# Batch 1's start in a spectral filter with a GELU layer: the filters' return, the weight sums and the tables at other places

## The chip, the cores and the metric

The kernel runs on one core of a Trainium2 chip. The metric is the device time of one execution in microseconds (us); lower is better. Before the change the median of three runs is 760.87 us (760.04 to 762.06).

## The reference

```python
X = np.fft.rfft(x, axis=1)                    # x: (8, 3008, 256)
Y = X * (filt_r + 1j * filt_i)[None, :, :]    # filters: (1505, 256)
y = np.fft.irfft(Y, n=3008, axis=1).astype(np.float32)
h = y.reshape(8 * 3008, 256) @ w_in           # w_in: (256, 2048)
g = 0.5 * h * (1.0 + erf(h / sqrt(2)))
out = g @ w_out                               # w_out: (2048, 256)
```

Each of eight batches is filtered along its 3008 positions in the frequency domain; the result then passes a layer of 2048 GELU units.

## The kernel before

**Two halves that run together.** The GELU layer works on 47 row tiles of 512 rows. Each tile has 16 slots; slot `s` belongs to tile `s // 16`. In every slot the loop at lines 865 to 872 first calls what the dictionary `at` holds for it, then one sixteenth of the previous tile's second product (`mm2` for the first and last tile, `mm2_seven` otherwise), then one sixteenth of this tile's first product (`mm1`, two matmuls of 512 columns and a GELU on ScalarE, ACT in the profile). Within each engine instructions run in the order in which the program issues them; no planner reorders them. So `put(slot, f, ...)` at lines 820 to 857 is the order of the work.

Batch 0 is filtered ahead of slot 0, by routines of its own. Batches 1 to 7 are filtered by calls that `put` has spread over the slots, one batch while the tiles of the one before go through the layer. Batch 1 must be ready at slot 80.

**The transform.** 3008 = 47 x 64, done in two stages each way:

- `s1` (four chunks of a batch): matmuls with table `T1s`; four evacuations into `a_sb` (three buffers); four DMA writes to the DRAM tile `R1` (R in the profile).
- `r1` (four chunks): reads `R1` back, transposed, into `b_sb` (three buffers), once all writes of `s1` have landed.
- `s2` (12 units `p`): two matmuls with `T2p`, then a product with the filter tile `F` on VectorE (DVE), 1024 elements wide. Unit p reads k = 2p and 2p + 1 of `F`. Below this product is called p(0) to p(11).
- `s3` and `s3_out` (three groups): inverse stage with table `U`, evacuated to `v_sb`, written to `R2`.
- `r2`, `s4`: read back as `d_sb`, last stage with table `T4a`, written to the ring `y_sb` that `mm1` reads.

**Filters.** Batch 0 needs `F` in one arrangement, the later batches in another. `save_filters` wrote `F` to the DRAM tile `Fd`; `load_filters_again` brings it back in the new arrangement, k = 0 to 7 as eight transfers of 128 KB (F1 below) and k = 8 to 23 as eight of 256 KB (F2). Each goes to 16 partitions. Units 0 to 3 read F1, units 4 to 11 F2.

**Queues.** All these transfers are issued by SyncE (SP) in program order. GpSimd (POOL) issues the loads of `x`, which `load_next` places at slot 25 for batch 2, and of `w_out`. It also computes tables: `table_2_parities` (`T2p`), `table_u_pick`, `table_4_rows`, `weights_4`, then the 24 products of `table_4_all` (`T4a`), which follow `table_4_factors` (three small matmuls and three evacuations on ACT).

**Seven products.** `mm2_seven` takes seven products of quarters in place of eight. For that it needs sums of quarters of `w_out` (`weight_sums`, into `w_sums`; once, before slot 36) and, per tile, sums of quarters of `g` (`sums_1`, `sums_2`, `sums_3` at lines 627, 633 and 640, on VectorE). The two PSUM banks `ps_o` are used in turn, and lines 670 to 680 read them on VectorE. Product m covers n = 16 m to 16 m + 15; slot s of a tile covers n = 7 s to 7 s + 6. Product m = 2 reads the sum of line 633, second half from n = 36.

For batch 1 the slots come from line 829: chunk c of `s1` at 0, 4, 8, 12, `r1` at 15, unit p of `s2` at 25 + 12 (p // 4) + int(2.5 (p % 4)), `r2` at 62, `s4` from 70.

Of the kernel before, what the change touches and what calls it, by code (L numbers as in the profile page):

```python
# [30 lines left out]
class _Mix:  # L31
# [343 lines left out]
    def s1(self, b, c):  # L375

        nc = self.nc
        if c == 0:
            self.st[b, "R1"] = self.dram.tile([NB, 48, 256], BF16, tag="R1", name="R1")
        a = self.pa.tile([128, 2, 4, 256], BF16, tag="a", name="a_sb")  # L380
        x = self.st[b, "x"]
        ps = [[self.bank("ps_s1", "h" if i == h == 0 else "f") for h in range(2)] for i in range(2)]
        for i in range(2):
            for r in range(2):
                for h in range(2):
                    w = 8 * c + 4 * r + 2 * i
                    nc.tensor.matmul(ps[i][h][64 * r:64 * r + 64, :], lhsT=self.T1s[64 * h:64 * h + NA],  # L387
                                     rhs=x[64 * h:64 * h + NA, w:w + 2, :], start=True, stop=True)
        for i in range(2):
            for h in range(2):  # L390
                self._evac(a[:, h, 2 * i:2 * i + 2, :].rearrange("p a b -> p (a b)"), ps[i][h], "act" if h else False)
        o = self.st[b, "R1"].rearrange("n q c -> q n c")
        for r in range(2):
            for h in range(2):
                w = HB * h + 8 * c + 4 * r
                nc.sync.dma_start(out=o[:, w:w + 4, :], in_=a[64 * r:64 * r + 48, h])
# [209 lines left out]
    def weight_sums(self):  # L606

        w = self.w_out_sb.rearrange("p (i k) (n o) -> p k n i o", k=2, n=2)
        q, tt = self.w_sums, self.nc.gpsimd.tensor_tensor
        for o, a, b, op in ((q[:, 0], w[:, 0, 1], w[:, 0, 0], ALU.subtract), (q[:, 1], w[:, 1, 1], q[:, 0], ALU.add),  # L610
                            (q[:, 2], w[:, 1, 1], w[:, 0, 1], ALU.add), (q[:, 3], w[:, 1, 0], q[:, 1], ALU.subtract)):
            for i in range(0, 8, 2):
                tt(out=o[:, i:i + 2], in0=a[:, i:i + 2], in1=b[:, i:i + 2], op=op)

    def quarters(self, t):

# [77 lines left out]
def kernel(  # L694
# [9 lines left out]
    m = _Mix(ctx, tc, x, filt_r, filt_i, moe_w_in, moe_w_out, out)  # L704
# [4 lines left out]
    g = m.small  # L709
    wide = ctx.enter_context(ExitStack())  # L710
    m.psum(wide, w=(2, 1), m=(1, 1), n=(5, 1))
    act = "act"
# [107 lines left out]
    def put(slot, f, *a):  # L820
        at.setdefault(slot, []).append((f, a))

    def first(b):
        return (b * S // TCH) * 16

    for b in range(1, B):
        hi = first(b)
        if b == 1:
            s1, n1, r1, s2, n2, group, r2, s4, n4 = 0, 4, 15, 25, 2.5, 12, 62, 70, 0.62
        else:  # L830
            s1, n1, r1, s2, n2, group, r2, s4, n4 = hi - 94, 3.7, hi - 80, hi - 71, 3.4, 14, hi - 25, hi - 17, 1
        unit = lambda p: s2 + group * (p // 4) + int(n2 * (p % 4))
        for u in range(16):
            put(s4 + int(u * n4), m.s4, b, u // 2, u % 2)
        for c in range(4):
            put(s1 + int(c * n1), m.s1, b, c)
            put(r1 if c < 3 else unit(3) + 1, m.r1, b, c)
            put(r2 if c < 3 else s4 + int(4 * n4) + 1, m.r2, b, c)
        for p in range(12):
            put(unit(p), m.s2, b, p)  # L840
            if p % 4 == 3:
                put(unit(p) + 3, m.s3, b, p // 4)
                put(unit(p) + 4, m.s3_out, b, p // 4, 1)
        if b + 1 < B:
            for i in range(8):
                put(unit(i + 2) if b > 1 else 25, m.load_next, b, i + 2, i // 2, i % 2)

    put(0, m.table_2_parities)
    put(1, m.table_u_pick, g)
    put(1, m.table_4_rows, g)  # L850
    put(1, m.weights_4, g)
    put(10, m.load_filters_again, 0, 8)
    put(16, m.load_filters_again, 8, 16)
    put(4, m.weight_sums)
    put(12, m.table_4_factors, g)
    put(14, m.table_u)
    put(15, m.table_4_all, g)
    seven = range(1, NT - 1)
    for t in seven:
        for i, s in enumerate((12, 13, 15, 17)):  # L860
# [43 lines left out]
```

## Time and profile before

| | TensorE | VectorE | ACT | GpSimd |
|---|---|---|---|---|
| busy, us of 758.5 | 741.2 | 581.4 | 547.6 | 111.6 |
| instructions | 8388 | 1043 | 967 | 207 |

| stretch, us | TensorE busy | VectorE busy | ACT busy | GpSimd busy | DMA share | GB/s |
|---|---|---|---|---|---|---|
| 38 to 52 (slots 0 to 15) | 11.20 of 14 | 6.09 | 12.95 | 7.54 | 1.09 | 203 |
| 52 to 64 | 9.93 of 12 | 0.99 | 6.38 | 11.84 | 0.84 | 184 |
| 64 to 82 | 17.45 of 18 | 13.22 | 10.01 | 17.06 | 1.02 | 164 |
| 82 to 98 | 13.17 of 16 | 15.32 | 8.66 | 6.00 | 0.88 | 212 |
| 98 to 114 | 15.09 of 16 | 12.54 | 11.13 | 0 | 0.33 | 81 |
| 300 to 500 | 199.80 of 200 | 161.68 | 148.77 | 15.12 | 0.49 | 119 |

A stretch is a piece of time counted from the start of the profiled execution. DMA share is the mean busy share of the 16 DMA engines; it can pass 1 a little where packets overlap. A matmul's end is modelled in the profile, so a TensorE that is busy throughout is not necessarily at its peak, but a gap in it is a gap. The profile numbers lines as the kernel before has them.

### The profile page before, as it was taken

To read this page: it belongs to the slowest core of one execution; us is meant where nothing else is said; L and a number is where in the kernel's file an instruction comes from. 1 tells how busy PE (TensorE), PEld (TensorE's weight loads), DVE (VectorE), ACT (ScalarE), POOL (GpSimd) and SP (SyncE) were. 2 spreads that over 40 slices of the span, in tenths; PEclk is the share of its full clock that TensorE was granted. 3 is DMA by queue.
4 is the path that set the end of the run, shared out by engine and by line. 5 is a ranking of instruction groups with operands and counts; after the bars stand their busy time and mean duration, and the time that the engine had idled before them with its cause. 6 is when DMAs were issued, how large, how long until landed. Compare 5 with 4: busy or idle time off the path is not lost.

```text
span 758.5 us, 20181 instructions
## 1 busy us (share of the span) xinstructions
PE 741.2 (98%) x8388; PEld 519.3 (68%) x8388; DVE 581.4 (77%) x1043; ACT 547.6 (72%) x967; POOL 111.6 (15%) x207
## 2 busy tenths in 40 slices
PE   8988899999999999999999999999999999999998
PEld 4835567666777667666677666766677766777776
DVE  7935888799677986889777897779977799666562
ACT  7885567766787677867778667876678767777773
POOL 7969600021000210002000120001200000000000
PEclk9999999999999999999999999999999999999999
DMA  9999935555624745347525465254562432501011
GB/s 147 221 191 172 197 107 130 148 120 124 140 78 126 159 112 113 100 131 169 119 75 141 139 132 127 79 165 111 105 168 65 140 92 81 129 29 57 29 57 57
DMA packets 91500, 90.71 MB, mean 120 GB/s; under 512 B 7632, under 2 KB 78416, under 8 KB 91088
## 3 DMA queue, kind: packets, MB, share of 16 engines
q1 hardware_dynamic: 83024, 73.43, 36.2%
q0 software_dynamic: 8384, 16.00, 13.9%
q8 instruction: 65, 1.06, 0.6%
q14 instruction: 27, 0.22, 0.1%
HBM read 57.15 MB, written 48.23 MB: 139 GB/s over the span
## 4 chain that ended last, share of the span: by engine, by line
PE 85%; DVE 7%; DMA 4%; issue 1%; ACT 1%; POOL 0%; SPq 0%; DVEq 0%; ACTq 0%; POOLq 0%
PE ps_h L569 38%; PE ps_o L657 35%; PE ps_s L455 3%; PE ps_s L427 2%; DVE p L413 2%; DVE s_sb L627 2%; PE ps_s L410 2%; PE ps_s L387 2%; DMA b_sb<-R 2%; PE ps_o L596 1%; DMA R<-a_sb 1%; DMA x_sb<-in_x_dram 1%; PE ps_c L517 1%; ACT y_sb L295 1%; DVE ost L680 1%
## 5 line engine op out<-in xcount | busy, mean ns | idle before, releaser
L572 ACT ACTIVATE g_sb<-ps_h 128x512 f16<-128x512 f32 x752 | 448.2, 599 | 191.1 <-PE ps_h L569 188.7
L569 PE MATMUL ps_h<-y_sb,w_in_sb 128*128 128x512 bf16 (+3 forms) x1600 | 448.2, 368 | 1.3 <-ACT g_sb L572 0.8
L657 PEld LDWEIGHTS <-g_sb 128*128 128x128 f16 x2880 | 190.3, 98 | 81.7 <-issue 16.9
L657 PEld LDWEIGHTS <-s_sb 128*128 128x128 f16 x2160 | 147.3, 98 | 51.3 <-issue 3.3
L569 PEld LDWEIGHTS <-w_in_sb 128*128 128x128 bf16 x1600 | 125.2, 98 | 9.3 <-issue 3.6
L657 PE MATMUL ps_o<-w_sums,g_sb 128*128 128x128 f16 x1440 | 125.0, 219 | 2.2 <-DVE t_sb L673 1.5
L657 PE MATMUL ps_o<-w_sums,s_sb 128*128 128x128 f16 x1440 | 124.5, 219 | 0.0
L627 DVE TENSOR_TENSOR s_sb<-g_sb 128x1024 f16<-128x1024 f16 x180 | 121.4, 697 | 0.0
L413 DVE TENSOR_TENSOR p<-ps_s,F 128x1024 bf16<-128x1024 f32 x84 | 102.6, 1221 | 23.2 <-PE ps_s L410 15.8
L657 PE MATMUL ps_o<-w_out_sb,g_sb 128*128 128x128 f16 x1440 | 118.4, 219 | 0.4
L118 POOL COPY gate<-p 1x1 bf16<-1x1 bf16 x40 | 19.4, 484 | 415.3 <-DVE p L413 415.3
L633 DVE TENSOR_TENSOR g_sb<-s_sb,g_sb 128x1024 f16<-128x1024 f16 x90 | 62.3, 693 | 1.1
L657 PE MATMUL ps_o<-w_out_sb,s_sb 128*128 128x128 f16 x720 | 62.2, 219 | 0.0
L640 DVE TENSOR_TENSOR s_sb<-g_sb 128x1024 f16<-128x1024 f16 x90 | 61.5, 683 | 0.0
L299 DVE TENSOR_SCALAR y_sb<-ps_s 128x376 bf16<-128x376 f32 x56 | 30.6, 546 | 28.9 <-PE ps_s L455 28.9
L297 DVE CAST a_sb<-ps_s 128x512 bf16<-128x512 f32 x56 | 36.1, 686 | 18.6 <-PE ps_s L387 15.4
L455 PEld LDWEIGHTS <-d_sb 96*128 96x128 bf16 x448 | 31.2, 98 | 26.4 <-issue 1.9
L675 DVE TENSOR_TENSOR t_sb<-t_sb,ps_o 128x256 f32<-128x256 f32 x45 | 18.7, 416 | 38.5 <-PE ps_o L657 38.5
L672 DVE TENSOR_TENSOR ost<-t_sb,ps_o 128x256 f32<-128x256 f32 x45 | 18.9, 419 | 31.2 <-PE ps_o L657 31.2
L680 DVE TENSOR_TENSOR ost<-t_sb,ps_o 128x256 f32<-128x256 f32 x90 | 33.7, 416 | 6.8 <-PE ps_o L657 6.8
L455 PE MATMUL ps_s<-T4a,d_sb 96*128 96x94 bf16 x448 | 37.1, 206 | 1.0 <-DMA d_sb<-R 0.9
L410 PE MATMUL ps_s<-b_sb,T2p 128*128 128x256 bf16 x168 | 32.3, 274 | 2.1 <-DMA b_sb<-R 2.1
(149 smaller groups left out, 524.3 us busy)
## 6 DMA issues: line engine op xcount, KB each, us to landing
out_dram<-ost SPq DMA_DIRECT2D x93, 256.0 KB, 2.7
x_sb<-in_x_dram POOLq DMA_DIRECT2D x64, 188.0 KB, 3.6
R<-a_sb SPq DMA_DIRECT2D x112, 96.0 KB, 2.2
b_sb<-R SPq DMA_DIRECT2D x28, 384.0 KB, 4.4
R<-v_sb SPq DMA_DIRECT2D x84, 128.0 KB, 2.4
d_sb<-R SPq DMA_DIRECT2D x56, 192.0 KB, 3.9
F<-Fd SPq DMA_DIRECT2D x8, 256.0 KB, 12.1
Fd<-F SPq DMA_DIRECT2D x1, 1536.0 KB, 9.9
```

The source lines that it names most:

```text
L297: self.nc.vector.tensor_copy(out=out, in_=in_)
L299: self.nc.vector.tensor_scalar(out=out, in0=in_, scalar1=scale, scalar2=None, op0=ALU.mult)
L410: nc.tensor.matmul(ps[:, 256 * i:256 * i + 256], lhsT=self.T2p[:, k].rearrange("p a b c d -> p (a b c d)"), rhs=self.st[b, "b", k // 6][:, ...
L413: nc.vector.tensor_tensor(out=w, in0=ps.unsqueeze(1).to_broadcast([128, 2, 512]), in1=self.F[:, :, 2 * p:2 * p + 2, :].rearrange("p t a b ...
L455: nc.tensor.matmul(ps[:, 94 * i:94 * i + 94], lhsT=d[:, (grp % 2) * 4 + i, 128 * half:128 * half + 128], rhs=self.T4a[:, 4 * grp + i], sta ...
L569: nc.tensor.matmul(ps[:, o:o + n], lhsT=self.w_in_sb[:, dc, jc * 128:jc * 128 + 128], rhs=self.ring[:, dc, off:off + n], start=(dc == 0), ...
L572: nc.scalar.activation(out=self.st["g", t][:, jc, :], in_=ps, func=AF.Gelu)
L627: self.nc.vector.tensor_tensor(out=self.st["s", t][:, i:i + 2], in0=a, in1=b, op=ALU.subtract)
L633: self.nc.vector.tensor_tensor(out=a21[:, k], in0=self.st["s", t][:, k, 0], in1=a22[:, k], op=ALU.add)
L640: self.nc.vector.tensor_tensor(out=self.st["s4", t][:, k], in0=a12[:, k], in1=s2[:, k], op=ALU.subtract)
L657: nc.tensor.matmul(ps[:, (m + 1) % 2, sub, :], lhsT=a[:, i, 128 * sub:128 * sub + 128], rhs=b[:, i], start=i == 0, stop=i == 7)
L680: v(out=c(h, 1 - h), in0=tt, in1=p, op=ALU.add)
```

## The change

It moves work of batch 1's start. F1 goes from slot 10, between the writes of chunks 2 and 3 of `s1`, to slot 13, behind all sixteen writes; F2 goes one slot later. `weight_sums` goes from GpSimd (16 pieces) to VectorE (4 whole ones) and from slot 4 to 17. In `s1` of batch 1 a third evacuation of each chunk goes from ACT to VectorE. GpSimd's small tables that the factors need come ahead of `T2p`, the factors go from slot 12 to 7 and `table_u` and `table_4_all` to 11. Forward and inverse stage of batch 1 start three slots earlier: `s2` at 22, `r2` at 59, `s4` at 67, the last a little more widely spread (0.75 slots apart instead of 0.62). It is for bringing the writes and the forward stage forward and for taking load off GpSimd and ACT.

```diff
-                self._evac(a[:, h, 2 * i:2 * i + 2, :].rearrange("p a b -> p (a b)"), ps[i][h], "act" if h else False)
+                self._evac(a[:, h, 2 * i:2 * i + 2, :].rearrange("p a b -> p (a b)"), ps[i][h],
+                           "act" if h and (b > 1 or i) else False)
...
-        q, tt = self.w_sums, self.nc.gpsimd.tensor_tensor
+        q, tt = self.w_sums, self.nc.vector.tensor_tensor
...
-            for i in range(0, 8, 2):
-                tt(out=o[:, i:i + 2], in0=a[:, i:i + 2], in1=b[:, i:i + 2], op=op)
+            tt(out=o, in0=a, in1=b, op=op)
...
-            s1, n1, r1, s2, n2, group, r2, s4, n4 = 0, 4, 15, 25, 2.5, 12, 62, 70, 0.62
+            s1, n1, r1, s2, n2, group, r2, s4, n4 = 0, 4, 15, 22, 2.5, 12, 59, 67, 0.75
...
+    put(0, m.table_4_rows, g)
+    put(0, m.weights_4, g)
+    put(0, m.table_u_pick, g)
     put(0, m.table_2_parities)
-    put(1, m.table_u_pick, g)
-    put(1, m.table_4_rows, g)
-    put(1, m.weights_4, g)
-    put(10, m.load_filters_again, 0, 8)
-    put(16, m.load_filters_again, 8, 16)
-    put(4, m.weight_sums)
-    put(12, m.table_4_factors, g)
-    put(14, m.table_u)
-    put(15, m.table_4_all, g)
+    put(7, m.table_4_factors, g)
+    put(11, m.table_u)
+    put(11, m.table_4_all, g)
+    put(13, m.load_filters_again, 0, 8)
+    put(17, m.load_filters_again, 8, 16)
+    put(17, m.weight_sums)
```

## The prediction, made before the changed kernel's time was known

> **What bounds the kernel now.** First the page: TensorE is busy for 741.2 of 758.5 us. Then the table of engines by stretch: from 126 us on TensorE is busy for the whole of nearly every stretch, until the last output, so there only fewer matmuls would help, and the change removes none. Its idle time lies ahead of that, where batch 1 is prepared beside the first row tiles. So I read the order of time of TensorE, VectorE and SyncE's queue in 38 to 126 us.
>
> ```profile
> 49.52 0.22 PE L351 MATMUL ps_t<-eye,T1g 47*96 47x47 bf16 x2 [1.89 <-ACT a_sb L295]
> 63.27 0.39 PE L410 MATMUL ps_s<-b_sb,T2p 128*128 128x256 bf16 x2 [2.07 <-DMA b_sb<-R]
> 85.42 0.38 PE L657 MATMUL ps_o<-w_sums,g_sb 128*128 128x128 f16 x4 [1.50 <-DVE t_sb L673]
> 97.16 0.51 PE L657 MATMUL ps_o<-w_sums,g_sb 128*128 128x128 f16 x6 [0.57 <-DVE g_sb L633]
> ```
>
> Columns: start, time, instruction, and in brackets the idle time before it and its releaser. With waits of 0.39, 0.39, 0.42, 0.76 (s3 on p) and 0.91 (s4 on d_sb) that is 8.9 us of waits. Two of them are followed by half clock, which the stretches show (third group: granted clock after ACT and POOL):
>
> ```profile
> 52.00:54.00 2.00, 2.00 (x8) 1.06 (x7) 0.00 (x0) 1.01 (x2) 2.00 (x4) 0.50 1.10 182
> 64.00:66.00 2.00, 2.00 (x9) 1.04 (x8) 0.93 (x1) 0.60 (x1) 1.84 (x4) 0.57 1.17 256
> ```
>
> Slots 25 to 27 take 63.5 to 68.0 instead of 2.8 us: about 1.7 us lost to the clock; the other about 1.6. What those waits hang on is SyncE's queue:
>
> ```profile
> 40.26 9.34 SPq L396 DMA_DIRECT2D R<-a_sb  x12
> 49.69 4.04 SPq L107 DMA_DIRECT2D F<-Fd  x8
> 53.83 2.76 SPq L396 DMA_DIRECT2D R<-a_sb  x4
> 59.99 1.29 SPq L402 DMA_DIRECT2D b_sb<-R  x3
> 61.38 4.63 SPq L107 DMA_DIRECT2D F<-Fd  x8
> ```
>
> The first part of the filters (F1) stands ahead of chunk 3's writes (R3). F1's first transfer is issued at 49.7 and lands after 4.0, at 53.7; the ninth transfer counted from it, R3's first, is issued at 53.8. The same holds for the ninth write of all, at 46.6 = 40.3 + 6.3. So at most eight are in flight. The second part (F2) lands last, and VectorE stands for it. Its last transfer (first line: issue; second: us to landing):
>
> ```profile
> L107 SPq DMA_DIRECT2D F<-Fd x1: 303/303/303, 65.7 to 65.7; - x1
> DMA to landing us min/median/max: 16.5/16.5/16.5
> ```
>
> In the order of time of VectorE:
>
> ```profile
> 82.57 1.23 DVE L413 TENSOR_TENSOR p<-ps_s,F 128x1024 bf16<-128x1024 f32 x1 [3.42 <-DMA out_dram<-ost]
> ```
>
> The profile puts that wait on an output store; the product p(4) reads k 8 and 9, and F2's last landing, 65.7 + 16.5 = 82.2, fits. The 1.50 us at 85.42 are its echo.
>
> **What the Trainium skill says.** "SBUF — State Buffer", section "Door 1: The DMA port swizzle": a transfer to 16 partitions reaches 4 of 16 ports and stays near 104 to 109 GB/s. F1 and F2 write 16 partitions each; the trace has 131 GB/s from 68 to 78, against 393 to 415 for b_sb (128 partitions): a little above the page, same sense. "DMA: Bandwidth & Descriptors", "Queues, rings and completion order": an engine takes its ring's descriptors in order and alternates between queues by packet. It agrees: R3, issued from 53.8, moves its small packets only from about 57.5, after F1. "TensorE: Matmul & The Clock Gate", "What's actually happening": an idle window of about 3.4 us halves the clock; here 2.07 us of waiting was enough, and 1.50 was not.
>
> **The change part by part.**
>
> *Order on SyncE.* Before: 12 writes, F1, R3, b, F2. Changed: 16 writes, F1, b, F2. R3 no longer queues behind F1, but F1 and then b queue behind R3. When can R3 go? Chunk 3's casts need chunk 0's a_sb buffer (three buffers), free when chunk 0's last write lands: 41.7 + 7.1 = 48.8. That landing is held by the loads of x and w_out in the other queue, not touched. Three casts on VectorE (0.6 each) end at 50.7; R3 is issued 50.9 to 52.2 and moved by 53.5. F1, issued from 52.7, then takes what it took before, 6.8 us (first packets 50.7, last 57.5): to about 60.4. b's first packets follow at 60.5 (before 61.0). b lands 2.2 us after its first packet (63.2 - 61.0): 62.7, a gain of 0.5. (The first product also reads F1: last packet 60.4, landed some 1.4 later, as 58.9 after 57.5, so ahead of b.) F2 ended 21.2 us after b's first packet (82.2 - 61.0): 81.7.
>
> *The three casts.* ACT loses 4 of 8 evacuations of 0.48 from start to start (1.9 us), VectorE gains 4 of 0.6; it is idle between chunks (1.35, 1.65, 3.08). With table_4_factors and table_u ahead of chunk 3 the 1.89 us wait goes as such, but the GELUs behind chunk 3's ACT cast still stand until 48.8. Slot 16 comes at about 50.5 instead of 52.42.
>
> *Weight sums.* GpSimd loses 16 of 0.635 (2.54 for four): 10.2 us, and 5.9 of waiting for w_out. VectorE gains 4 of 1024 f16; nearest row L640, 0.68: 2.7 us, inside its idle 9.77 us before 59.94. Cost nothing. GpSimd's table_4_all (59.7 to 83.9 now) starts when the factors are cast, about 44.8, and takes 8 groups of 2.73: to about 66.6. It is needed at slot 67: no gain on the path. But batch 2's eight x loads, behind it on GpSimd (now 83.9 to 88, after F2), start at 66.6, beside F2. Cost to F2: from 0 (its ports are its limit, the engines have room) to all their own time, 8 us (85.5 to 93.5 now); an even packet for packet gives 13 x packets of 0.25 us per engine, 3. I take 1: F2 ends at 82.7.
>
> *Slots 25 to 22.* Slot 22 is reached at 50.5 + 6 x 0.87 = 55.7, and s2 there waits for b until 62.7: 7 us, then half clock, 1.7. Before, 25 slots were done at 63.3; now 22 at 62.7; the later slots' mm2, mm1 and GELUs queue behind. Three slots (2.6) less in front of the wait against 0.5 gained: 2 us behind. The 2 us gained in slots 0 to 15 are inside this wait.
>
> *F2's wait, moved.* p(4) now stands at slot 34, in the changed kernel's instruction order on VectorE ahead of sums_2 (L633) and of the bank's copy L670. Slot 37 (mm2_seven, n = 36) reads the sum's second half. So TensorE stops at 37. In the kernel before p(4) came behind both; TensorE ran on until slot 43, where product m = 5 needs a bank that L672 and L673, behind p(4), had yet to read. Without that stop it would be there 16.8 us after b (ten slots of 0.87, five of 0.82, six s2 of 0.22, s3 1.0, half clock 1.7): 79.5. It goes on at 82.7 + 1.15 (p) + 0.65 (L633) = 84.5: 5.0 us. Behind the stopped matmul stands all of TensorE's stream, mm1 too, so ACT's GELUs stop with it. Then slots 37 to 44 as before without their 0.42 and 1.50: 86.07 - 77.33 - 1.92 = 6.8, and half clock again, 1.7: slot 44 at 93.0 against 86.07, 6.9 later. Behind it the waits of 0.76 and 0.57 should go, since VectorE stands nearer to TensorE after this stop; 0.91 stays (r2 to s4 is still eight slots). Sum: 6.9 - 1.3 = **5.6 us slower**, 766.5.
>
> The last slots: s4 spread by 0.75 from 67 ends at 78, before 80 as now; chunk 3's b, behind F2 in the queue, lands near 84.6 and is read at slot 48, after 93. Neither costs. Rearranging GpSimd's small tables costs nothing: both orders end near 43.8, before anything reads them but the factors (slot 7, about 43).
>
> **The rivals.** *Milder*: no half clock after the second stop, F2 undisturbed, ending at 81.7: 5.6 - 1.7 - 1.0 = 2.9 slower, 763.8. For it: 1.50 us did not bring it; against: 5 us is more than 2.07. *The x loads delay F2 by 5*: 5.6 + 4 = 9.6, 770.5. For it: they do share the engines; against: F2 is limited by its ports. *Faster*: the filters return at 200 GB/s, as the stretch 51 to 53 shows for F1 mixed with writes. F1 takes 5, b lands at 60.9, F2 (2 MB in 10 us) ends at 71.6, before p(4). Then 0.2 us behind at slot 28, and 0.42, 1.50, 0.76 and 0.57 go: about 3 faster, 757.8. Against it: 131 GB/s for 14 us on end. *Level*: F2 ends at 78.5 (some 150 GB/s): TensorE waits 0.8 at slot 37, without half clock, slot 44 at 87.1 is 1.0 late, less 1.3: 760.6. Against it the same 131 GB/s.
>
> **How the numbers follow.** Forecast 0.53, milder 0.17, delayed x 0.12, faster 0.10, level 0.08. The time is the forecast's, 766.5. The range takes in milder and delayed x, and most of level: 760.5 to 771. Slower by over 0.3% (above 763.2): 0.53 + 0.17 + 0.12, less a little of the milder case, 0.80; within 0.10; faster 0.10.
>
> **What would show it.** Right: SyncE issues 16 writes on end, R3 near 51 to 52; b lands near 62.7; the first s2 shows 5 to 7 us of waiting; p(4) waits on VectorE until 82 to 84; the L657 matmul of slot 37 is released by L633 after about 5 us. Wrong: b there by 58, or F2 all landed before 78, or no wait at slot 37.

## The result and the profile after

| | median, us | range, us | runs |
|---|---|---|---|
| before | 760.75 | 760.04 to 762.06 | 4 |
| changed | 766.16 | 765.31 to 767.05 | 4 |

The ratio is 1.0069, with a 95% interval of 1.0051 to 1.0087: the change makes the kernel about 5.4 us slower. The forecast was 766.5, 5.6 slower.

TensorE's order of time, changed kernel; these are all its waits of more than 0.35 us between 38 and 128 us (lines between 391 and 611 of the kernel before count one more here):

```profile
49.18 1.02 PE L570 MATMUL ps_h<-y_sb,w_in_sb 128*128 128x512 bf16 x4 [1.09 <-DVE a_sb L297]
...
63.39 0.58 PE L411 MATMUL ps_s<-b_sb,T2p 128*128 128x256 bf16 x2 [7.98 <-DMA b_sb<-R]
...
86.70 0.82 PE L657 MATMUL ps_o<-w_sums,g_sb 128*128 128x128 f16 x6 [5.98 <-DVE g_sb L633]
```

Nine waits have become three. TensorE now stands still twice for long: 8 us for `b_sb` at the first `s2`, and 6 us at slot 37 for a sum of `g` (L633) that stands behind p(4) on VectorE. SyncE's queue:

```profile
40.47 11.70 SPq L397 DMA_DIRECT2D R<-a_sb  x16
52.26 3.67 SPq L107 DMA_DIRECT2D F<-Fd  x8
56.02 2.12 SPq L403 DMA_DIRECT2D b_sb<-R  x3
58.77 7.69 SPq L107 DMA_DIRECT2D F<-Fd  x8
```

Sixteen writes on end, then F1, b, F2, as the order in the program has it. Chunk 3's writes go out by 52.2 (before: 56.6), yet b (the reads of `R1` into `b_sb`) is issued only 4 us earlier than before and lands no sooner (63.3 against 63.2), since it now stands behind F1. F2's last transfer, issue and us to landing, and VectorE behind it:

```profile
L107 SPq DMA_DIRECT2D F<-Fd x1: 303/303/303, 66.2 to 66.2; - x1
DMA to landing us min/median/max: 18.3/18.3/18.3
```

```profile
84.82 1.22 DVE L414 TENSOR_TENSOR p<-ps_s,F 128x1024 bf16<-128x1024 f32 x1 [6.71 <-issue]
85.96 0.68 DVE L633 TENSOR_TENSOR g_sb<-s_sb,g_sb 128x1024 f16<-128x1024 f16 x1
```

With two decimals that is 66.16 + 18.28 = 84.44: p(4) starts 0.4 later, the sum ends at 86.6, and TensorE goes on at 86.70. The profile gives "issue" as what p(4) waited for; the landing is what fits. The stretches of 2 us after both stops (granted clock is the third number from the end):

```profile
64.00:66.00 2.00, 1.78 (x8) 1.11 (x8) 1.22 (x1) 0.28 (x1) 1.92 (x3) 0.50 1.37 239
66.00:68.00 2.00, 2.00 (x12) 1.23 (x11) 1.02 (x2) 0.89 (x2) 1.92 (x3) 0.67 1.01 123
...
86.00:88.00 2.00, 1.30 (x8) 0.92 (x9) 2.00 (x4) 0.00 (x0) 0.00 (x0) 0.50 1.07 250
88.00:90.00 2.00, 2.00 (x12) 1.22 (x11) 1.54 (x4) 0.60 (x1) 0.00 (x0) 0.50 1.03 250
```

Half clock after each. Busy time multiplied by the clock that is missing, with the stretches next to these (62 to 64: 0.61 us at 0.50; 90 to 92: 2.00 at 0.70), gives 1.85 us lost after the first stop and 2.25 after the second. By stretch, TensorE's busy time (a microsecond at half clock counts in full):

| stretch, us | before | changed |
|---|---|---|
| 38 to 52 | 11.20 | 12.79 |
| 52 to 64 | 9.93 | 4.02 |
| 64 to 82 | 17.45 | 16.39 |
| 82 to 98 | 13.17 | 11.20 |
| 98 to 114 | 15.09 | 15.84 |

The first chunks do go faster, by 1.6 us; the stretch of the first stop takes that and 4.3 more, the two after it 3.0; the last gives 0.75 back.

### The profile page after: what moved, and what is told of

It reads as the page before. It is cut to its first block, busy times and chain, and to the rows that moved or that the text cites. A ratio compares the mean times of both kernels' runs of the same rounds, so it can differ in the third digit from the quotient of the medians.

```text
span 765.3 us, 20030 instructions
## 1 busy us (share of the span) xinstructions
PE 733.2 (96%) x8252; PEld 520.0 (68%) x8388; DVE 585.7 (77%) x1051; ACT 545.5 (71%) x963; POOL 101.1 (13%) x191
## 4 chain that ended last, share of the span: by engine, by line
PE 79%; DMA 8%; DVE 4%; issue 3%; POOL 2%; ACT 2%; SPq 1%; DVEq 0%; POOLq 0%; ACTq 0%
PE ps_o L657 35%; PE ps_h L570 33%; PE ps_s L456 3%; PE ps_s L428 3%; PE ps_s L411 2%; DMA F<-Fd 2%; ACT g_sb L573 2%; PE ps_s L387 2%; DVE p L414 2%; DMA x_sb<-in_x_dram 2%; DVE s_sb L627 1%; DMA b_sb<-R 1%; DMA R<-v_sb 1%; DMA d_sb<-R 1%; DMA F<-in_filt_i_dram 1%
## 5 line engine op out<-in xcount | busy, mean ns | idle before, releaser
L570 PE MATMUL ps_h<-y_sb,w_in_sb 128*128 128x512 bf16 (+3 forms) x1468 | 419.7, 366 | 1.2 <-DVE a_sb L297 1.1
L627 DVE TENSOR_TENSOR s_sb<-g_sb 128x1024 f16<-128x1024 f16 x180 | 118.7, 682 | 0.0
L633 DVE TENSOR_TENSOR g_sb<-s_sb,g_sb 128x1024 f16<-128x1024 f16 x90 | 61.7, 686 | 1.1
L640 DVE TENSOR_TENSOR s_sb<-g_sb 128x1024 f16<-128x1024 f16 x90 | 61.3, 681 | 0.0
L297 DVE CAST a_sb<-ps_s 128x512 bf16<-128x512 f32 x60 | 38.5, 685 | 16.8 <-PE ps_s L387 13.9
```

Source lines behind the costliest of these rows:

```text
L297: self.nc.vector.tensor_copy(out=out, in_=in_)
L570: nc.tensor.matmul(ps[:, o:o + n], lhsT=self.w_in_sb[:, dc, jc * 128:jc * 128 + 128], rhs=self.ring[:, dc, off:off + n], start=(dc == 0), ...
L627: self.nc.vector.tensor_tensor(out=self.st["s", t][:, i:i + 2], in0=a, in1=b, op=ALU.subtract)
L633: self.nc.vector.tensor_tensor(out=a21[:, k], in0=self.st["s", t][:, k, 0], in1=a22[:, k], op=ALU.add)
L640: self.nc.vector.tensor_tensor(out=self.st["s4", t][:, k], in0=a12[:, k], in1=s2[:, k], op=ALU.subtract)
```

## The experiments

All times are medians. The kernel before was run beside each group of them and measured 760.78, 761.15 and 761.48 us in these, so between groups the ratios are compared.

### Which part costs: the slots, or the order on SyncE

The theory: two stops cost the time, one for b and one for F2, both because the forward stage is asked for earlier than its data can come. The rival: the new order on SyncE (or the work moved to VectorE) does it, and the slots cost nothing.

**The slots alone**, put on the kernel before:

```diff
-            s1, n1, r1, s2, n2, group, r2, s4, n4 = 0, 4, 15, 25, 2.5, 12, 62, 70, 0.62
+            s1, n1, r1, s2, n2, group, r2, s4, n4 = 0, 4, 15, 22, 2.5, 12, 59, 67, 0.75
```

> The kernel before with one edit: batch 1's forward and inverse stage at the changed slots (s2 at 22, r2 at 59, s4 at 67). Theory A (the earlier slots put the two waits for the filters and b in front of more work of TensorE): b lands at 63.2 as before, slot 22 waits for it 4 to 5 us and is then three slots behind; p(4) stands ahead of the sum of line 633, F2 lands at 82.2, so slot 37 waits until about 84 for 3 to 4 us; 764 to 767 us, nearly the whole loss. Theory B (the order on SyncE, F1 between all writes and b, delays b and F2): nothing of that is in this kernel, 760 to 761.5. Theory C (x loads beside F2 through the free GpSimd): also 760 to 761.5.

Measured: 764.53, ratio 1.0047 (1.0031 to 1.0064). TensorE's order of time (its two long stops at b and at F2):

```profile
63.54 0.61 PE L410 MATMUL ps_s<-b_sb,T2p 128*128 128x256 bf16 x2 [4.87 <-DMA b_sb<-R]
85.01 0.82 PE L657 MATMUL ps_o<-w_sums,g_sb 128*128 128x128 f16 x6 [3.92 <-DVE g_sb L633]
```

The slots alone bring both stops, at the same two places, and 3.7 of the 5.4 us.

**All of the change but the slots** (that edit turned round, in the changed kernel):

> The changed kernel with the slots of before (s2 at 25, r2 at 62, s4 at 70), all else changed. Theory A: the first s2 still starts at about 63.3, but with 25 slots done as in the kernel before; F2 lands at about 84.5 as in the changed kernel, 2.3 later than before, and p(4) holds up slot 43 instead of 37: 1.5 us of waiting there becomes 3 to 4; 762 to 764. Theory B or C: the slots do not matter, 765.5 to 767.

Measured: 762.88, ratio 1.0034 (1.0023 to 1.0045). It waits 5.60 us for b and stops once more:

```profile
89.67 0.40 PE L657 MATMUL ps_o<-w_sums,g_sb 128*128 128x128 f16 x4 [4.71 <-DVE t_sb L673]
```

This is the place of the 1.50 us in the kernel before (slot 43, the bank that L673 must have read), three times as long: F2's last transfer lands at 66.85 + 19.78 = 86.63, and p(4) starts at 87.0. So the rest of the change costs about 2 us by itself, and in this trace it shows as a later F2. 3.7 and 2.1 add up to 5.8, about the 5.4 of the whole. Which part of the rest delays F2 is shown only in part: the order on SyncE and the loads of `x` have runs of their own below; the casts and weight sums on VectorE and the order of GpSimd's tables were not run alone.

**The order on SyncE alone**, on the kernel before:

```diff
-    put(10, m.load_filters_again, 0, 8)
-    put(16, m.load_filters_again, 8, 16)
+    put(13, m.load_filters_again, 0, 8)
+    put(17, m.load_filters_again, 8, 16)
```

> The kernel before with one edit: F1 at slot 13 behind all sixteen writes, F2 at slot 17. Theory A: R3 goes at about 52 instead of 55, F1 then takes its 7 us, b lands within 0.5 us of before (63.2) and F2 too: 760 to 761.5. Theory B: b and F2 come 1 to 2 us later and TensorE with them, 762 to 763. If bringing R3 forward paid as meant: b at 61 or earlier, 758 to 759.5.

Measured: 760.55, ratio 0.9996 (0.9986 to 1.0006): level. TensorE's waits, this kernel:

```profile
61.19 0.39 PE L410 MATMUL ps_s<-b_sb,T2p 128*128 128x256 bf16 x2 [2.57 <-DMA b_sb<-R]
...
83.24 0.44 PE L657 MATMUL ps_o<-w_sums,g_sb 128*128 128x128 f16 x4 [2.46 <-DVE t_sb L673]
...
111.64 0.51 PE L455 MATMUL ps_s<-T4a,d_sb 96*128 96x94 bf16 x8 [1.01 <-DMA d_sb<-R]
```

and the last of these in the kernel before:

```profile
113.71 0.51 PE L455 MATMUL ps_s<-T4a,d_sb 96*128 96x94 bf16 x8 [0.91 <-DMA d_sb<-R]
```

In this profiled run TensorE is past b 2 us earlier than in the kernel before (61.2 against 63.3), F2 lands 2 us earlier too (80.1 against 82.2), and at d_sb TensorE is still 2.1 us ahead, although it waits 2.46 instead of 1.50 us for the echo of F2. But the profiled run is the fastest of the 22, 1.9 us under their median, so its trace cannot say what a median run gains or loses at these stops. The medians say that the order alone neither gains nor costs.

### Is it F2, and is it p(4)'s place

**No F2 at all** in the changed kernel; it leaves out the return of the filters for k = 8 to 23, and units 4 to 11 multiply by what stands in `F`:

```diff
-    put(17, m.load_filters_again, 8, 16)
```

> The changed kernel without F2: the filters of k 8 to 23 are not brought back, so units 4 to 11 of the later batches multiply by the arrangement of batch 0. Theory A: p(4) waits for no transfer, the wait at slot 37 goes, the wait of the first s2 (for b, behind F1) stays at 7 to 8 us; 759.5 to 762. If the loss came from TensorE's half clock or VectorE's load instead: 764 to 766.

Measured: 758.15, ratio 0.9958 (0.9943 to 0.9972), lower than expected. One long wait is left:

```profile
63.10 0.59 PE L411 MATMUL ps_s<-b_sb,T2p 128*128 128x256 bf16 x2 [7.97 <-DMA b_sb<-R]
```

The stop for b is as long as in the changed kernel, and yet this is faster than the kernel before. F2's landing costs the changed kernel some 8 us (766.16 - 758.15, 1.1% by the ratios): the 5.98 of the stop and the half clock after it. With the stop for b alone, 7.97, a wait of 0.72 ahead of it and some 2.3 of half clock make 11.0 us, against 8.9 of waits and 3.3 of half clock in the kernel before, which still has its own wait for F2.

**p(4) and its followers three slots later**, units 0 to 3 as in the change:

```diff
-        unit = lambda p: s2 + group * (p // 4) + int(n2 * (p % 4))
+        unit = lambda p: s2 + group * (p // 4) + int(n2 * (p % 4)) + (3 if b == 1 and p > 3 else 0)
```

with `r2` and `s4` at the slots of before.

> The changed kernel, units 0 to 3 of s2 at the changed slots, units 4 to 11 and all behind them (r2, s4) at the slots of before, so that p(4) stands at slot 37 again, behind the sum of line 633. Theory A (the greater part of the slots' cost is p(4) in front of that sum, the smaller the three slots not done before b): the 8 us wait of the first s2 stays, the 6 us wait at slot 37 goes, slot 43 waits for 1 to 2 us; 760.5 to 763. Rival A2 (the cost is the first wait, three slots earlier): 764.5 to 766.

Measured: 763.2, ratio 1.0036 (1.0026 to 1.0046), just above what was expected. The stop at slot 37 is gone, but five waits of 0.48 to 1.13 us come in its place (on a bank that L673 reads, on p, on v_sb, on the sums, on d_sb); F2 lands at 84.1, about as late as in the changed kernel (84.4). Moving the consumer without bringing the data gives half of it back.

**The x loads out of F2's way**: the changed kernel, with the loads of batch 2's `x` held back until p(4) is there, that is, until F2 has landed.

```diff
-        if b > 1:
+        if True:
...
-                put(unit(i + 2) if b > 1 else 25, m.load_next, b, i + 2, i // 2, i % 2)
+                put(unit(i + 2) if b > 1 else unit(4), m.load_next, b, i + 2 if b > 1 else 4, i // 2, i % 2)
```

> The changed kernel with one edit: the x loads of batch 2 are held on GpSimd until product p(4) is there, so they start behind F2. Theory A with the x loads as a small addition: F2 lands 2 us earlier (82.3 instead of 84.5), slot 37 goes on 2 us earlier, 763.5 to 764.5. Theory C (the x loads are the main cause): 760.5 to 762. If F2 is limited by its ports alone: no change, 765.5 to 766.5.

Measured: 764.66, ratio 1.0046 (1.0028 to 1.0064). The interval overlaps that of the change, so the times alone leave it open. F2 does not land 2 us earlier in this trace, as was expected: the first write starts 2.9 us later than in the changed kernel (43.3 against 40.5), and F2 lands at 84.4 in both. What the x loads cost is seen better inside F2, at its last two transfers, beside which they move. In the changed kernel these two land 5.5 us after the sixth (78.9 to 84.4); in this run, without x loads beside them, 4.1, and in the kernel before 4.1 too. That is 1.4 us for the x loads. It is not the same in every run: two other traces with x loads beside F2 (the slots of before, and p(4) three slots later) give 6.7 and 4.7 us in place of 5.5.

### What would bring F2 sooner

**Half of the return by GpSimd's queue** (par = 1 of F1 and F2, issued at slot 9 ahead of `table_4_all`; par = 0 stays on SyncE), once with the slots of before, once with the changed ones (of the edit, the calls):

```diff
-    put(13, m.load_filters_again, 0, 8)
-    put(17, m.load_filters_again, 8, 16)
+    put(9, m.load_filters_again, 0, 8, 1, nc.gpsimd)
+    put(9, m.load_filters_again, 8, 16, 1, nc.gpsimd)
+    put(13, m.load_filters_again, 0, 8, 0, nc.sync)
+    put(17, m.load_filters_again, 8, 16, 0, nc.sync)
```

> The changed kernel with the slots of before (s2 at 25, r2 at 62, s4 at 70) and the filters' return split on two queues: the half for partitions 64 to 127 is issued by GpSimd at slot 9, ahead of table_4_all, the other half by SyncE as in the changed kernel. Theory A with the ports as F's limit: the halves use different ports and run side by side, SyncE's F1 takes 3.5 us instead of 7 to 8, b lands at 59 to 60.5, F2 by 72, no wait for p(4); 754.5 to 757.5. If the engines and not the ports limit F: the same bytes take the same time, b at 62 to 63.5 and F2 at 82 or later, 761 to 764.

> The changed kernel, its own slots, with the return split on two queues as in the run beside it. Theory A: the wait at slot 37 goes, the first s2 waits from about 55.4 to 59 or 60.5; 755 to 758, level with or up to 1.5 us above the same split at the slots of before. If the engines limit F: 764 to 767.

Measured: 759.68, ratio 0.9979 (0.9971 to 0.9988), and 760.03, ratio 0.9987 (0.9977 to 0.9996). No stop at F2 in either. Between these two kernels only the slots differ, and the ratios differ by 0.08%, with overlapping intervals; between the changed kernel and the same with the slots of before they differ by 0.35% (1.0069 and 1.0034). So the earlier slots cost where F2 is late, and nothing clear where it is not. Both are slower than expected, though, since SyncE's writes are starved by the half in the other queue (first of the two kernels; from 50 to 54 us SyncE's queue has 6 and 12% of the engines' time, GpSimd's 100%):

```profile
41.05 17.61 SPq L397 DMA_DIRECT2D R<-a_sb  x16
```

17.6 us instead of 11.7; b lands at about 65.6 and TensorE waits 7.82 for it. The halves moved after one another, not side by side, so this told nothing of what limits the rate.

**Wider transfers.** F1 and F2 go to 16 partitions a transfer. In "SBUF — State Buffer", section "Door 1: The DMA port swizzle", the Trainium skill says that the rate depends on how many of 16 ports the partitions of one transfer reach: 16 partitions reach 4 (about 109 GB/s at best), 32 reach 8 (218), 128 all 16 (436). If that is what limits F2, wider transfers of the same bytes must be faster; if the reading of DRAM or the descriptors do, they are not. For this `Fd` is saved in the order in which it is read back:

```diff
-        self.nc.sync.dma_start(out=self.Fd, in_=self.F[0:64])
+        for par in range(2):
+            for q in range(2):
+                o = 32 * par + 16 * q
+                self.nc.sync.dma_start(out=self.Fd[o:o + 16], in_=self.F[32 * q + (par ^ q):32 * q + 32:2])
...
-                for q in range(2):
-                    o = 64 * par + 32 * r + 16 * q
-                    self.nc.sync.dma_start(out=self.F[o:o + 16, :, k0:k0 + k, :],
-                                           in_=self.Fd[32 * q + (par ^ q):32 * q + 32:2, :, k0:k0 + k, :])
+                o = 64 * par + 32 * r
+                self.nc.sync.dma_start(out=self.F[o:o + 32, :, k0:k0 + k, :],
+                                       in_=self.Fd[32 * par:32 * par + 32, :, k0:k0 + k, :])
```

> The changed kernel, with the filters' return in transfers to 32 partitions instead of 16: the save writes Fd in the order in which it is read back (four transfers instead of one), and the return takes four transfers for each of F1 and F2 instead of eight, with the same bytes and the same descriptors. Theory (the return is limited by the partitions, so the ports, that one transfer reaches): F1 takes about 4.5 us instead of 7.5 to 8, b lands near 60, F2 moves at about twice 130 GB/s and ends near 70; p(4) does not wait, TensorE's stop at slot 37 goes, the wait for b is about 5 us. The kernel without F2 took 758.2 with b at 63.1, so 755 to 758. Rival (the return is limited by what does not depend on the width of a transfer, the reading of DRAM or the descriptors): F2 stays at about 130 GB/s, ends at 84, 765 to 767.

The order of the rows in DRAM changes with this (adjacent rows are read in place of every second one).

For 128 partitions `Fd` holds every row twice (eight saving transfers, 3 MB), and F1 and F2 are one transfer each (of the edit, the return):

```diff
+        self.nc.sync.dma_start(out=self.F[:, :, k0:k0 + k, :], in_=self.Fd[:, :, k0:k0 + k, :])
```

> The changed kernel, with the filters' return in one transfer of 1 MB (F1) and one of 2 MB (F2), each to all 128 partitions. Fd is saved in the order of the return, twice over in DRAM (eight transfers and 3 MB instead of one and 1.5 MB, from 22 us on). Theory (ports): b_sb came at 393 to 415 GB/s to 128 partitions, so F1 takes about 3 us, b lands near 58.5, F2 (2 MB) ends near 66; the wait for b is 3 to 4 us, no stop at slot 37: 753 to 757, unless the longer save delays the loads of x and w_out behind it (up to 4 us more). Rival (width does not matter): F2 at 130 GB/s as before, 765 to 767.

> The kernel before, with the filters' return to 128 partitions as in the run beside it. Theory (ports): F1 is through in 3 us, chunk 3's writes go where they went or a little earlier, b lands near 60 to 61, F2 ends near 70: the waits of 2.07 (b) and 1.50 (echo of F2) go, with the half clock after the first: 755 to 758. Rival: 760 to 762.

> The kernel before with the changed order on SyncE (F1 at slot 13, behind all sixteen writes, F2 at 17) and the return to 128 partitions. That order alone was level (760.6), since the gain at b was given back at F2. Theory (ports): F2 no longer takes it back, b lands near 57 to 58, ahead of slot 25 (58.6): no wait there, none at F2: 752 to 756. If b is not the first to be gained, because the loads of x and w_out set the start of the writes, it equals the run on the kernel before with the same return. Rival: 760 to 761.

| return of the filters | rest of the kernel | us | ratio to before |
|---|---|---|---|
| 32 partitions | changed | 754.85 | 0.9919 (0.9907 to 0.9931) |
| 128 partitions | changed | 757.39 | 0.9954 (0.9932 to 0.9977) |
| 128 partitions | before | 758.63 | 0.9963 (0.9954 to 0.9972) |
| 128 partitions | before, changed order on SyncE | 757.37 | 0.9952 (0.9938 to 0.9965) |

A stretch of 2 us in which F2 is nearly all that moves, in the changed kernel, in that with 32 and in that with 128 partitions (last number: GB/s):

```profile
72.00:74.00 2.00, 1.95 (x15) 1.38 (x15) 1.87 (x3) 1.19 (x2) 0.00 (x0) 1.00 1.01 123
```

```profile
66.00:68.00 2.00, 2.00 (x10) 1.15 (x9) 1.23 (x1) 0.46 (x2) 1.92 (x3) 0.55 1.01 217
```

```profile
66.00:68.00 2.00, 1.78 (x8) 1.11 (x8) 1.02 (x1) 0.50 (x1) 1.84 (x4) 0.50 1.04 439
```

123, 217, 439 GB/s, and the DMA share (the number ahead) is 1 in all three: the engines look full at every rate. The rate goes with the width, as the page says; 217 and 439 are its figures within 1%, while 123 lies above its 109. The wider transfers are also larger, but that is not the reason: F1 with 32 partitions moves in transfers of 256 KB, as large as those of F2 with 16, and has 221 GB/s where those have 123:

```profile
56.00:58.00 2.00, 0.50 (x3) 0.01 (x1) 0.45 (x1) 0.86 (x2) 1.92 (x2) 1.00 1.03 221
```

Nor can the order of the rows be all of it: from 32 to 128 partitions it stays adjacent, and the rate doubles again. What it adds from 16 to 32 was not tested.

With 32 partitions F2 has landed at 73.6 instead of 84.4; p(4) does not wait, and the only waits left are these:

```profile
50.27 1.02 PE L572 MATMUL ps_h<-y_sb,w_in_sb 128*128 128x512 bf16 x4 [1.17 <-DVE a_sb L299]
61.77 0.58 PE L413 MATMUL ps_s<-b_sb,T2p 128*128 128x256 bf16 x2 [5.27 <-POOL t_sb L373]
```

(The profile names a table of GpSimd for the second. b's first chunk, issued at 56.0, lands 5.6 us later, at 61.6, which fits the end of the wait.) This is the best version of all, faster than both kernels.

With 128 partitions F2 is faster still, and the kernel is not: the longer save, from 21 to some 40 us, runs into the loads of batch 1's `x` and of `w_out`. The eight loads of that `x` take 13.4 us from issue to landing (median), against 6.6 in the changed kernel. Changed kernel, 128 partitions:

```profile
40.61 0.37 PE L386 MATMUL ps_s<-x_sb,T1s 47*64 47x512 bf16 x1 [1.97 <-DMA x_sb<-in_x_dram]
42.56 1.06 PE L386 MATMUL ps_s<-x_sb,T1s 47*64 47x512 bf16 x7 [1.57 <-DMA x_sb<-in_x_dram]
```

3.5 us of new waits for `x`, and the first write starts at 45.1 instead of 40.5. All three of these runs end later than expected (753 to 757, 755 to 758, 752 to 756). In the last of them the wait for b is gone, as was expected, but 1.22 us for `x` and 1.49 for `w_out` have come, and 1.59 for a_sb is left (1.89 in the kernel before). Its expectation says that the order alone had lost at F2 what it gained at b; the trace of that order, above, does not show this.

What was not tried: the 32-partition return on the kernel before, and with the changed order alone. So how much of the 0.8% needs the rest of the change is not known.

## Why the prediction was right

**The bound and the part of it that moves.** Right. Two landings, b and F2, decide; the slots make TensorE arrive earlier at both. That the slots, and not the order on SyncE, carry most of it is shown by the runs of either alone (3.7 us and none). That F2 is what makes them costly is shown by the run without F2 and by the two with half of F2 on the other queue.

**Order on SyncE.** F1 was said to take 6.8 us and end at 60.4. It took 7.5 to 8: it moves at 139 to 143 GB/s in 56 to 60 and ends at about 61.5, and b lands at 63.3, not 62.7. Of the gain of 0.5 nothing came. In the run with this order alone F1 moved at about 150 GB/s and b was there at 61.1, so F1's pace is not the same in all kernels; why is open. That R3 would be issued by about 52.2, the sixteen writes on end, and slot 16 at 50.5 (50.04) hold.

**The casts and the weight sums.** Right as to the path: the wait at chunk 3 shrank from 1.89 to 1.09 us, and the weight sums lie in VectorE's idle time. But the sums took not 2.7 but 4.65 us; only one of the four took the 0.68 of the row that was used:

```profile
50.24 0.68 DVE L613 TENSOR_TENSOR w_sums<-w_out_sb 128x1024 f16<-128x1024 f16 x1
50.95 1.20 DVE L613 TENSOR_TENSOR w_sums<-w_out_sb,w_sums 128x1024 f16<-128x1024 f16 x1
52.08 1.46 DVE L613 TENSOR_TENSOR w_sums<-w_out_sb 128x1024 f16<-128x1024 f16 x1
```

They run beside `table_4_all` on GpSimd, whose pairs of products took 2.15 to 2.38 us then and 1.60 at 64.8. VectorE was free until 64.0, so it cost nothing.

**Slots 25 to 22.** Slot 22 was reached at 55.4 (55.7 said), the wait was 7.98 us (7.0), and the half clock after it cost 1.85 (1.7).

**F2's wait, moved.** The place, slot 37, the releaser, L633, and the half clock are as said. F2 landed at 84.4, not 82.7. Of these 1.7 us, 0.6 come from b, which landed at 63.3 instead of 62.7. From there F2 took 21.2 us, 2.2 more than the 19.0 of the kernel before, where the forecast allowed 1 for the x loads: 1.4 lie in the last two transfers, beside which x moves, and 0.8 in the first six, which came more slowly (123 instead of 131 GB/s) with almost no x beside them. That slower pace was not in the forecast, and its reason is open. Another 0.4 us passed between F2's landing and the start of p(4), which the forecast put at nothing (it was 0.4 in the kernel before too, 82.2 to 82.57). The wait was 5.98, not 5.0, the half clock cost 2.25, not 1.7, and slot 44 came at 95.1, not 93.0.

**The sum.** At slot 44 the changed kernel is 9.0 us behind (95.1 - 86.07), where 6.9 was forecast; then the waits of 0.76, 0.57 and also the 0.91 for d_sb go, where 0.91 was to stay: 9.0 - 2.2 = 6.8, which is the difference of the two profiled spans, 765.3 - 758.5. The medians differ by 5.4. So by its own trace the forecast of 5.6 was 1.2 too small: F2's landing and the step from it to p(4) were put 2.1 too early, the gain behind was put 0.9 too small. The nearness of 766.5 to 766.16 is partly luck: the two errors offset each other in part, and single runs stray from their median, the profiled one by 0.9 us here and by up to 3.1 in the other kernels (760.45 against 757.39).

**The rivals.** Milder falls: the clock did halve. x by 5 us falls: 1.4. Faster and level both asked for a quicker return of the filters, 150 to 200 GB/s; in the changed kernel it was 123 to 143. With 32 partitions it is 217, and the time then is 754.85, where the rival said 757.8 for 200. Its mechanism was right; what it lacked was the quicker return, and wider transfers brought that.

The last chunk of b landed at 91.8, not 84.6 (behind F2 and the x loads); it is read at 99.6 and cost nothing.

## What to carry to other kernels

Before a consumer is moved earlier, ask when the slowest thing it reads lands, and what stands in front of that in its queue: here an earlier forward stage only lengthened two waits, and it cost nothing clear once the slowest transfer came by another way. When a transfer is what everyone waits for, look at its rate before its place: here 123 GB/s at a DMA share of 1 was the mark of transfers to 16 partitions, and the same bytes in transfers to 32 gave 217 GB/s and a kernel 0.8% faster than before instead of 0.7% slower. The widest form is not always the best: here it needed twice the bytes saved, in a stretch where other loads had no room.

## What was not expected of the hardware

**A newcomer in the other queue waits.** In the changed kernel GpSimd issues the x loads from 67.4:

```profile
67.41 4.18 POOL L86 DMA_DIRECT2D x_sb<-in_x_dram  x8
```

From 68 to 76 only the queue of SyncE (q1) shows packets. Queue table, packets, MB and share of 16 engines, for 78 to 80 us:

```profile
q1 hardware_dynamic: 28, 0.13, 58.4%
q0 software_dynamic: 33, 0.14, 53.2%
```

So the x loads moved 10 us after their issue, and only then were shared out evenly. The prediction took the Trainium skill's turn by turn between queues ("DMA: Bandwidth & Descriptors", "Queues, rings and completion order") as holding from the start; the trace shows it only for the tail of F2. In the run without F2, where VectorE did the same products at these times, the x loads issued at 67.4 moved at once, and the first landed at 71.6 instead of 83.6; so it is F2 that they stand behind. Why they stand back so long was not tested.

**Half clock is not a matter of the one wait's length.** In the run with the order on SyncE alone, 2.57 us of waiting for b at 58.6 to 61.2 was followed by full clock and 2.46 us at 80.8 to 83.2 by a low one (stretches of 4 us):

```profile
62.00:66.00 4.00, 4.00 (x30) 2.66 (x28) 3.27 (x4) 2.39 (x4) 3.76 (x5) 1.00 1.15 188
...
82.00:86.00 4.00, 2.76 (x17) 1.84 (x18) 3.97 (x7) 0.60 (x1) 2.97 (x6) 0.68 1.03 178
```

What decides was not tested.
